# Five buffers instead of four for the weight tiles of a fused attention and feed-forward kernel

## The chip, the cores and the metric

The kernel runs on one core of a Trainium2 chip. The metric is the device time of one launch in microseconds (us); lower is better. Times of the kernel before are given as the median of three runs, and one further execution was recorded by the hardware profiler.

## What is computed

Two stages are fused. First, attention with 8 batches, 8 heads, 576 positions and a head width of 64, in which each query keeps only its 32 highest scores:

```python
scores = scale * np.matmul(q, k.transpose(0, 1, 3, 2))
kth = np.partition(scores, -top_k, axis=-1)[..., -top_k:-top_k + 1]
scores = np.where(scores >= kth, scores, -1000000000.0)
attn = np.exp(scores - np.max(scores, axis=-1, keepdims=True))
attn = attn / (np.sum(attn, axis=-1, keepdims=True) + 1e-09)
out = np.matmul(attn, v)
```

Then its output, regarded as 4608 tokens of width 512, goes through a gated feed-forward layer with an inner width of 1536:

```python
gate = 1.0 / (1.0 + np.exp(-(x @ w_gate)))
val = x @ w_val
return (gate * val @ w_out).astype(np.float32)
```

## The kernel before

**Attention.** The work is cut into steps: a batch, a pair of heads and a block of 128 queries (the last block of a head pair holds the 64 left-over positions of both heads). There are 160 steps. `scores` (line 221) lets TensorE multiply keys and queries into the PSUM tiles `pss` (L239, or L269 in batch 0), and ScalarE copies them to `s`. `select` (line 321) finds each row's 32nd highest score: VectorE takes maxima (L338, L342, L366) and writes the masked numerators `e` (L292). `turn` (line 371) transposes `e` on TensorE into `pt` (L378), 9 transposes of 128 columns for a full step. `weigh` (line 390) multiplies with the values into `po`: L414 and L424 write only half of the array's columns each (the tile `128*64` in the trace), one half per head, and L428 all of them (`128*128`). L431 adds the reciprocals of the sums, and the quotient is split into a high and a low part, `xh` and `xl`.

**Feed-forward.** Whenever the four head pairs of a unit of 256 or 384 tokens are there, `ffn` (line 451) queues tasks for it. `wide` (line 466) multiplies one 128-wide slice of `w_gate` and `w_val` with the tokens: 24 matmuls, L475 to L477, into two PSUM tiles `pz`. `narrow` (line 487) multiplies a slice of `w_out` in 12 matmuls, L496 to L498, into `po` (named `po2` in the program). A unit has 12 `wide` and 12 `narrow` tasks in three groups.

**Weights.** Each weight is kept as a high and a low part. `split_weights` (line 115) makes these parts once, for 18 tiles of 1 MB (8 KB in each of 128 partitions): VectorE and ScalarE prepare them, TensorE forms the remainder (`wrest`, L168 to L170), ScalarE writes it to the tile (`w_split`, L163 and L171), and SyncE writes the tile to device memory (`ws`, L172). The first two units use some of these tiles straight from on-chip memory; all others are read again by `load` in `ffn`:

```python
wt = pools["w"].tile([P, 2, 2, NP, P], F32R, tag="w", name=f"w_{nm0}_{idx}")
nc.sync.dma_start(wt.rearrange("p i a c n -> p i a (c n)").bitcast(F32), w_split[idx])
```

That is L461, 222 loads. Both `split_weights` and `load` take their tiles from the pool `w`, which `ffn_pools` (line 111) makes. A tile is handed out again when the last matmul that reads it is done, so the number of buffers sets how many weight tiles can be in use or under way.

**Order.** All engines run their instructions in order. The kernel writes steps and tasks in an order of its own (the loop in `run`), and the framework's scheduler then sorts the instructions of every engine by priority and by when it expects their operands and buffers to be ready. So a change of a pool's size can move instructions on every engine. SyncE issues nearly all DMAs in one queue: queries (L211, L208), keys (L192), values (L202), weights (L461) and outputs (L504); an issue that waits for a buffer holds up those behind it.

At the end a flag is formed on TensorE and VectorE (`n_bad`, L664, and `flag`, L666) and read by every engine (L667); only if it is set is everything computed again in a general way.

Of the kernel before, what the change touches and what calls it, by code (L numbers as in the profile page):

```python
# [30 lines left out]
def tile_topk_attention_then_gated_ffn(  # L31
# [19 lines left out]
    FG = NE = NP  # L51
# [57 lines left out]
    pools, fresh, copies, ahead, requests = {"first": bkr}, {}, [], [], []  # L109

    def ffn_pools():
        for name, bufs in (("w", 4), ("f2", 3), ("f4", NE), ("fg", FG + 1)):
            pools[name] = ctx.enter_context(tc.tile_pool(name=name, bufs=bufs))

    def split_weights():
# [401 lines left out]
    def run(general):  # L517
# [27 lines left out]
        if not general:  # L545
            ffn_pools()
            splits = split_weights()
# [176 lines left out]
```

## Time and profile before

| | |
|---|---|
| median of 3 runs | 1564.49 us |
| lowest, highest run | 1562.36, 1564.89 us |
| profiled execution, its own time | 1562.55 us |
| its span from first to last instruction | 1560.7 us |
| TensorE matmuls, busy | 1510.3 us (97%) |
| VectorE, busy | 1284.5 us (82%) |
| ScalarE, busy | 1116.0 us (72%) |
| GpSimd, busy | 1063.5 us (68%) |
| DMA queue q1, share of the 16 engines | 62.5% |
| granted TensorE clock, mean | 0.993 |

In the trace PE is the stream of matmuls on TensorE, PEld its weight loads, DVE VectorE, ACT ScalarE, POOL GpSimd, and SPq the DMA issues of SyncE. Matmuls follow each other in a pipeline, so that one's recorded time overlaps the next one's: the pace of TensorE is read from the distance between the starts of two matmuls, not from their durations.

### The profile page before, as it was taken

To read this page: it belongs to the slowest core of one execution; us is meant where nothing else is said; L and a number is where in the kernel's file an instruction comes from. 1 tells how busy PE (TensorE), PEld (TensorE's weight loads), DVE (VectorE), ACT (ScalarE), POOL (GpSimd) and SP (SyncE) were. 2 spreads that over 40 slices of the span, in tenths; PEclk is the share of its full clock that TensorE was granted. 3 is DMA by queue.
4 is the path that set the end of the run, shared out by engine and by line. 5 is a ranking of instruction groups with operands and counts; after the bars stand their busy time and mean duration, and the time that the engine had idled before them with its cause. 6 is when DMAs were issued, how large, how long until landed. Compare 5 with 4: busy or idle time off the path is not lost.

```text
span 1560.7 us, 33841 instructions
## 1 busy us (share of the span) xinstructions
PE 1510.3 (97%) x10586; PEld 1378.4 (88%) x10586; DVE 1284.5 (82%) x5806; ACT 1116.0 (72%) x2405; POOL 1063.5 (68%) x1756
## 2 busy tenths in 40 slices
PE   6779999999999999999999999999999999999998
PEld 2346689999999999899999999999999999999998
DVE  7999868999988789888988879988898888888311
ACT  8998968787877687776776766777777777677221
POOL 4666658898766786787666876787766886676211
PEclk8999999999999999999999999999999999999999
DMA  7763598887655755566555665565564675465574
GB/s 251 258 222 134 214 359 314 290 282 291 230 187 200 245 197 206 182 229 221 204 178 198 223 239 189 195 238 196 208 223 168 208 250 194 173 223 177 193 273 158
DMA packets 88894, 344.14 MB, mean 220 GB/s; under 512 B 9856, under 2 KB 36992, under 8 KB 57984
## 3 DMA queue, kind: packets, MB, share of 16 engines
q1 hardware_dynamic: 88560, 341.58, 62.5%
q8 instruction: 86, 1.41, 0.4%
q14 instruction: 104, 0.85, 0.2%
q10 hardware_dynamic: 144, 0.29, 0.1%
HBM read 313.52 MB, written 28.31 MB: 219 GB/s over the span
## 4 chain that ended last, share of the span: by engine, by line
PE 74%; DVE 9%; POOL 6%; ACT 6%; issue 2%; DMA 2%; SPq 0%; POOLq 0%; ACTq 0%
PE pz L476 11%; PE pz L477 11%; PE pz L475 11%; PE pss L239 8%; PE po L414 6%; PE pt L378 6%; PE po L496 5%; PE po L498 5%; PE po L497 5%; POOL u L356 3%; DVE cand L338 2%; DVE e L292 2%; PE po L428 2%; ACT e L287 2%; ACT under L350 1%
## 5 line engine op out<-in xcount | busy, mean ns | idle before, releaser
L356 POOL TENSOR_TENSOR u<-s,under 128x288 f32<-128x288 f32 x576 | 456.0, 814 | 138.1 <-ACT under L350 127.4
L338 DVE MAX8 cand<-s 128x8 f32<-128x72 f32 x2304 | 346.6, 217 | 64.6 <-ACT s L246 56.3
L475 PE MATMUL pz<-xh,w 128*128 128x384 f32 (+1 forms) x1184 | 390.4, 332 | 1.1 <-DVE acc L502 0.7
L477 PE MATMUL pz<-xh,w 128*128 128x384 f32 (+1 forms) x1184 | 391.1, 331 | 0.0
L476 PE MATMUL pz<-xl,w 128*128 128x384 f32 (+1 forms) x1184 | 390.1, 330 | 0.3 <-POOL xl L448 0.3
L292 DVE SCALAR_TENSOR_TENSOR e<-s,kths,e 128x576 f32<-128x576 f32 x288 | 280.7, 977 | 0.9 <-ACT e L287 0.7
L350 ACT ACTIVATE under<-s,leads 128x576 bf16<-128x576 f32 x288 | 222.6, 774 | 80.4 <-DVE leads L342 33.1
L366 DVE MAX8 kths<-u 128x8 f32<-128x584 f32 x288 | 219.1, 761 | 45.0 <-POOL u L357 43.3
L287 ACT ACTIVATE e<-s,st 128x576 f32<-128x576 f32 x288 | 209.6, 771 | 62.9 <-POOL st L346 62.4
L483 POOL TENSOR_TENSOR gl<-gf,gh 128x384 fp32r<-128x384 f32 (+1 forms) x156 | 151.6, 972 | 116.5 <-ACT gh L482 112.7
L475 PEld LDWEIGHTS pz<-xh,w 128*128 128x128 f32 x1184 | 222.8, 189 | 2.4 <-DVE acc L502 1.0
L476 PEld LDWEIGHTS pz<-xl,w 128*128 128x128 f32 x1184 | 223.3, 189 | 0.8 <-POOL xl L448 0.6
L477 PEld LDWEIGHTS pz<-xh,w 128*128 128x128 f32 x1184 | 223.1, 189 | 0.3
L379 ACT ACTIVATE et<-pt 128x384 f32<-128x384 f32 x384 | 177.9, 486 | 27.9 <-PE pt L378 26.0
L496 PE MATMUL po<-gh,w 128*128 128x384 f32 (+1 forms) x592 | 194.6, 334 | 0.7 <-DVE acc L502 0.6
L497 PE MATMUL po<-gl,w 128*128 128x384 f32 (+1 forms) x592 | 194.9, 330 | 0.0
L498 PE MATMUL po<-gh,w 128*128 128x384 f32 (+1 forms) x592 | 194.3, 330 | 0.0
L246 ACT ACTIVATE s<-pss 128x576 f32<-128x576 f32 x252 | 161.2, 640 | 41.3 <-PE pss L239 40.5
L378 PE MATMUL pt<-ident,e 128*128 128x128 f32 x1152 | 179.6, 274 | 7.9 <-ACT et L379 4.2
L239 PE MATMUL pss<-k,qh 128*128 128x288 f32 (+2 forms) x588 | 164.9, 298 | 1.5 <-ACT s L246 1.5
L378 PEld LDWEIGHTS pt<-ident,e 128*128 128x128 f32 x1152 | 140.9, 141 | 24.6 <-ACT et L379 6.4
L239 PE MATMUL pss<-k,ql 128*128 128x288 f32 (+2 forms) x588 | 159.9, 294 | 0.0
(108 smaller groups left out, 2897.3 us busy)
## 6 DMA issues: line engine op xcount, KB each, us to landing
w<-ws SPq DMA_DIRECT2D x222, 1024.0 KB, 5.0
v<-in_v_dram SPq DMA_DIRECT2D x68, 352.0 KB, 3.2
wraw<-in_w_dram SPq DMA_DIRECT2D x36, 512.0 KB, 4.9
ws<-w_split SPq DMA_DIRECT2D x18, 1024.0 KB, 4.6
qraw<-in_q_dram SPq DMA_DIRECT2D x140, 128.0 KB, 3.1
kraw<-in_k_dram SPq DMA_DIRECT2D x56, 288.0 KB, 4.0
out_dram<-acc SPq DMA_DIRECT2D x40, 192.0 KB, 4.8
out_dram<-acc SPq DMA_DIRECT2D x12, 128.0 KB, 5.3
```

What stands on the lines that cost most here:

```text
L239: nc.tensor.matmul(ps[:, half, o : o + n], x[:, h * P : (h + 1) * P], ks[h][:, k0 : k0 + n], start=t == 0, stop=t == len(todo) - 1,)
L287: nc.scalar.activation(e[:, j], s[:, j], AF.Exp, bias=st[:, j : j + 1], scale=1.0 / SHRINK)
L292: nc.vector.scalar_tensor_tensor(e[:, j], s[:, j], kth[j], e[:, j], op0=ALU.is_ge, op1=ALU.mult, accum_out=st[:, 4 + j : 5 + j])
L338: nc.vector.max(cand[:, j, 8 * g : 8 * g + 8], s[:, j, g * SEG : (g + 1) * SEG])
L356: nc.gpsimd.tensor_tensor(u[:, j, part], s[:, j, part], under[:, j, part], op=ALU.mult)
L378: nc.tensor.transpose(pt[:, c], ef[:, k0 : k0 + P], ident)
L475: nc.tensor.matmul(ps, wt[:, u, 0, d], xh, start=d == 0, stop=False)
L476: nc.tensor.matmul(ps, wt[:, u, 0, d], xl, start=False, stop=False)
L477: nc.tensor.matmul(ps, wt[:, u, 1, d], xh, start=False, stop=d == NP - 1)
L496: nc.tensor.matmul(ps, wt[:, e % 2, 0, f], gh, start=f == 0, stop=False)
L497: nc.tensor.matmul(ps, wt[:, e % 2, 0, f], gl, start=False, stop=False)
L498: nc.tensor.matmul(ps, wt[:, e % 2, 1, f], gh, start=False, stop=f == FG - 1)
```

## The change

```diff
     def ffn_pools():
-        for name, bufs in (("w", 4), ("f2", 3), ("f4", NE), ("fg", FG + 1)):
+        for name, bufs in (("w", 5), ("f2", 3), ("f4", NE), ("fg", FG + 1)):
             pools[name] = ctx.enter_context(tc.tile_pool(name=name, bufs=bufs))
```

The pool `w` gets a fifth buffer, 8 KB more in each partition. The scratch of the dynamic DMAs is 1024 bytes in both kernels (`dynamic_dma_scratch_size=1024`), so this line is the whole difference in the code. All engines have the same instructions before and after, 9464 on TensorE, 4945 on VectorE, 2121 on ScalarE, 1761 on GpSimd and 620 on SyncE on the path that is taken; the scheduler orders them differently.

SyncE, in the last batch but one, number 6 (`w` are weight loads, `qraw`, `kraw` and `v` loads of queries, keys and values, `ws` the split weights in device memory). Before:

```order
L211 DMA qraw_4_1_18468<-in_q_dram 128x256
L461 DMA w_9_19263<-ws_132 128x2048
L202 DMA v_0_18892<-in_v_dram 128x704
L211 DMA qraw_3_2_18619<-in_q_dram 128x256
L461 DMA w_10_19408<-ws_133 128x2048
L461 DMA w_11_19526<-ws_134 128x2048
L211 DMA qraw_4_2_18772<-in_q_dram 128x256
L461 DMA w_0_19671<-ws_123 128x2048
```

Now:

```order
L461 DMA w_9_19263<-ws_132 128x2048
L211 DMA qraw_4_1_18468<-in_q_dram 128x256
L461 DMA w_10_19408<-ws_133 128x2048
L461 DMA w_11_19526<-ws_134 128x2048
L211 DMA qraw_3_2_18619<-in_q_dram 128x256
L202 DMA v_0_18892<-in_v_dram 128x704
L461 DMA w_0_19671<-ws_123 128x2048
L211 DMA qraw_4_2_18772<-in_q_dram 128x256
```

The weight loads stand a place or two further ahead among the other loads.

TensorE, in `weigh` for queries 2 and 3 of head pair 0 in batch 0 (tile `po_3_0`; `pz_1_3` are the matmuls of the first feed-forward unit around it). Before, the eight half-column matmuls are one run:

```order
L170 MATMUL wrest_0_1462<-wt_frac_1455,plus 128x512
L414 MATMUL po_3_0_1676<-et_2_0_1526,v_0_1158 64x256 x8
L428 MATMUL po_3_0_1676<-et_2_0_1526,v_0_1158 128x256
L431 MATMUL po_3_0_1676<-ident,inv_2_0_1220 128x128
L431 MATMUL po_3_0_1676<-ident,inv_3_0_1316 128x128
```

Now they alternate with feed-forward matmuls, to the eighth:

```order
L414 MATMUL po_3_0_1676<-et_2_0_1526,v_0_1158 64x256
L475 MATMUL pz_1_3_0_1419<-xh_2_1061,w_split_1023 128x256
L414 MATMUL po_3_0_1676<-et_2_0_1526,v_0_1158 64x256
L476 MATMUL pz_1_3_0_1419<-xl_2_1062,w_split_1023 128x256
L414 MATMUL po_3_0_1676<-et_2_0_1526,v_0_1158 64x256
L477 MATMUL pz_1_3_0_1419<-xh_2_1061,w_split_1023 128x256
L414 MATMUL po_3_0_1676<-et_2_0_1526,v_0_1158 64x256
L475 MATMUL pz_1_3_0_1419<-xh_3_1237,w_split_1023 128x256
```

One run of eight has become eight runs of one.

TensorE, at the transposes of batch 5, block 1, head pair 3 (`pt_5_1_3`; `pss_5_3_0_1` are scores of a later step). Before:

```order
L477 MATMUL pz_8_0_0_1_15912<-xh_8_2_14188,w_8_0_15895 128x384
L378 MATMUL pt_5_1_3_0_15650<-ident_105,e_5_1_3_15246 128x128 x3
L378 MATMUL pt_5_1_3_1_15655<-ident_105,e_5_1_3_15246 128x128 x3
L239 MATMUL pss_5_3_0_1_15113<-k_11_0_1_13823,qh_5_3_0_14809 128x288
L239 MATMUL pss_5_3_0_1_15113<-k_11_0_1_13823,ql_5_3_0_14810 128x288
```

Now:

```order
L498 MATMUL po2_7_2_2_16146<-gh_7_2_3_15862,w_7_17_16144 128x384
L239 MATMUL pss_5_3_0_1_15113<-k_11_0_1_13823,qh_5_3_0_14809 128x288
L239 MATMUL pss_5_3_0_1_15113<-k_11_0_1_13823,ql_5_3_0_14810 128x288
L239 MATMUL pss_5_3_0_1_15113<-k_11_0_1_13823,qh_5_3_0_14809 128x288
L239 MATMUL pss_5_3_0_1_15113<-k_11_0_1_13823,ql_5_3_0_14810 128x288
L378 MATMUL pt_5_1_3_0_15650<-ident_105,e_5_1_3_15246 128x128 x3
L378 MATMUL pt_5_1_3_1_15655<-ident_105,e_5_1_3_15246 128x128
```

Other feed-forward work stands ahead of these transposes than before. Between the last score matmul of the step and its first transpose there were 94 matmuls, 59 of them feed-forward and 12 scores; now there are 83, with 44 and 16.

## Rows read from the trace of the kernel before

**Rows 1.** Stretches of 40 us: busy PE, PEld, DVE, ACT, POOL; clock; DMA share, GB/s.

```profile
120.00:160.00 40.00, 38.54 (x244) 27.11 (x242) 38.81 (x179) 35.27 (x73) 26.22 (x42) 1.00 0.39 130
160.00:200.00 40.00, 36.23 (x238) 27.42 (x237) 35.63 (x104) 36.51 (x66) 22.57 (x33) 1.00 0.55 205
200.00:240.00 40.00, 38.75 (x329) 34.69 (x329) 25.83 (x122) 24.22 (x55) 25.84 (x47) 1.00 1.01 384
...
1480.00:1520.00 40.00, 40.00 (x233) 40.00 (x232) 4.88 (x9) 8.33 (x17) 6.09 (x6) 1.00 0.77 267
```

**Rows 2.** Waits of PE: line, awaited engine and line; us in total, times, longest.

```profile
PE wrest L168 <- DVE wt_lead L153: 8.2, 7, 3.5
...
PE pss L269 <- DMA k<-in_k_dram: 4.1, 1, 4.1
PE pt L378 <- DVE e L292: 3.6, 6, 1.0
...
PE pz L477 <- ACT w_split L171: 1.6, 1, 1.6
```

**Rows 3.** Waits of SyncE's queue: the weight loads on feed-forward matmuls.

```profile
SPq L461 <- PE pz L477: 282.6, 97, 7.2
```

**Rows 4.** The weight tiles' page: the 222 loads, from issue to landing.

```profile
DMA to landing us min/median/max: 4.7/5.0/11.0
```

**Rows 5.** Timeline, 211 to 224 us: start, us, what.

```profile
211.78 6.08 SPq L461 DMA_DIRECT2D w<-ws  x4
...
223.40 0.28 PE L475 MATMUL pz<-xh,w 128*128 128x256 f32 x1
```

**Rows 6.** Timeline of PE, 131 to 134 us.

```profile
131.26 1.95 PE L414 MATMUL po<-et,v 128*64 128x256 f32 x16
133.14 0.70 PE L428 MATMUL po<-et,v 128*128 128x256 f32 x2
```

**Rows 7.** Timeline of PE, 871 to 873 us.

```profile
871.42 0.20 PE L239 MATMUL pss<-k,qh 128*128 128x64 f32 x1
871.55 0.65 PE L414 MATMUL po<-et,v 128*64 128x256 f32 x2
872.13 0.30 PE L239 MATMUL pss<-k,ql 128*128 128x64 f32 x1
872.36 1.08 PE L414 MATMUL po<-et,v 128*64 128x256 f32 x6
```

**Rows 8.** The chain that ended last, 120 to 215 us: start, us, what.

```profile
131.33 1.88 PE po L414 x16
...
163.77 0.94 ACT w_split L163
...
187.39 1.68 DVE wt_frac L162
```

**Rows 9.** Timeline, 985 to 1002 us: step of batch 5, block 1, head pair 3.

```profile
985.14 0.29 PE L239 MATMUL pss<-k,qh 128*128 128x288 f32 x1
985.27 0.30 PE L239 MATMUL pss<-k,ql 128*128 128x288 f32 x1
...
986.47 0.33 PE L476 MATMUL pz<-xl,w 128*128 128x384 f32 x1
986.64 0.33 PE L477 MATMUL pz<-xh,w 128*128 128x384 f32 x1
...
999.49 1.36 DVE L292 SCALAR_TENSOR_TENSOR e<-s,kths,e 128x576 f32<-128x576 f32 x1
...
1001.36 0.60 PE L378 MATMUL pt<-ident,e 128*128 128x128 f32 x4
...
1002.13 0.33 PE L378 MATMUL pt<-ident,e 128*128 128x128 f32 x1 [0.18 <-DVE e L292]
```

**Rows 10.** Timeline of SyncE at the end: the four last output DMAs.

```profile
1552.58 3.34 SPq L504 DMA_DIRECT2D out_dram<-acc  x4
```

## The prediction

> **What bounds the kernel now.** I read the stretches first. From 280 us to the end matmuls fill the time: the stretch of 1480 to 1520 us shows TensorE busy for 40.00 of 40 us, while VectorE needs 4.88 [rows 1]. Over the whole span TensorE is busy for 97%. So the time is the sum of TensorE's work at its pace plus the few places where it stands still. Between 120 and 240 us, where the weights are split and the first units start, it is idle for 1.46, 3.77 and 1.25 us, 6.5 in all [rows 1]. Before 120 us VectorE is the busier one; the two programs are alike there but for a few rows.
>
> Then I read what TensorE waits for [rows 2]. Of the DMAs it waits for one, a load of keys, 4.1 us, once. No weight load stands among its waits. The rest are short: 8.2 us on the preparation of the split weights, 3.6 us on masked numerators `e`, 1.6 us on a split tile.
>
> SyncE does wait for weight buffers: 97 times, 282.6 us in total, for the last matmul of an older tile [rows 3]. That is the wait that a fifth buffer shortens. The question is whether anybody on the path feels it.
>
> **The change part by part.**
>
> *The fifth buffer itself: 0 us.* A weight load takes 5.0 us in the median and 11.0 at most [rows 4]. The tightest one that I find, pairing the order of the loads with the first matmul on each tile, is issued at 211.78 us, the first of four in its row; even with the longest landing time it is there by 222.8 us, and its matmul starts at 223.40, right behind other matmuls [rows 5]. That is where the DMA engines are full, share 1.01 [rows 1]; later loads have more room. So loads issued one buffer earlier land earlier and wait in memory. What hides this term is the lead of four buffers that is already there. Queries and keys now stand a place or two further behind in SyncE's queue; they cost nothing as long as TensorE shows no wait on them, and it shows none but the 4.1 us at the start.
>
> *The eight half-column matmuls that now alternate with feed-forward matmuls, 3.6 us of TensorE.* This is what the scheduler does with the changed sizes, and it is the one place where TensorE's pace changes. I counted the runs of half-column matmuls in both programs: 82 before, 89 now, and all seven of the difference are here, where one run of eight became eight of one; elsewhere it is 81 and 81, in other places. In a run, eight such matmuls (16 in the trace, two passes each) take from 131.26 to 133.14 us, 1.88 us [rows 6]: two halves of the array work side by side. A lone one is to be seen at 871.55: the next matmul starts 0.58 us later, at 872.13, and the one after that, a matmul of 64 columns, is followed after 0.23 us, where its like at 871.42 is followed after 0.13 [rows 7]. So a lone one costs 0.58 + 0.10 = 0.68 us, eight of them 5.44, and 5.44 − 1.88 = 3.6 us more.
>
> How much of this reaches the end? At 131 us the chain that ended last runs through TensorE, through this very run, but at 164 us through ScalarE and at 187 us through VectorE [rows 8], and TensorE has 6.5 us of idle time there to lose [rows 1]. The ends are 0 (all taken out of that idle time) and 3.6 (none, since ScalarE and VectorE wait for TensorE in turn). The chain is on TensorE for about as much of this stretch as on the others, so I take half: **+1.8 us**.
>
> The Trainium skill, "TensorE: Matmul & The Clock Gate", section "Single matmul latency", gives a constant of about 166 ns at the full clock for a matmul that can't hide its drain, and "TensorEngine Tiling (Array Packing)", section "Key Properties", says that a change of the tiling mode drains the array. By these, seven more runs would cost an estimated 1.2 us, a third of what the rows give; halved, the sum below would be 1.2 us smaller. The lone run at 871.55 agrees that there is a drain; it shows besides that a half without its partner costs time, and I go by it.
>
> *Transposes that come nearer to their scores: +0.8 us.* TensorE can transpose `e` only when VectorE, ScalarE and GpSimd have finished the selection. In the step of the third order excerpt the last scores start at 985.27 us, the numerators of the first head are done at 999.49 + 1.36 = 1000.85, and the first transpose starts at 1001.36, 0.5 us later; the fifth, of the second head, waits 0.18 us [rows 9]. Now 15 fewer feed-forward matmuls lie between, at 0.17 us (986.47 to 986.64), and 4 more scores at 0.13 us (985.14 to 985.27): 2.6 − 0.5 = 2.1 us less, and with 0.5 us in hand a wait of 1.6 us. The same sum over all 160 steps finds ten that fall short, the first at 122 us and the last at 1381, the worst being this one; together 7 us. They come in five clusters of neighbouring steps, and as VectorE runs on while TensorE waits, I count only the worst of each: 4.4 us. From this the 3.6 us that TensorE waits for `e` now [rows 2] go off, as those steps have got more room. The ends are −3.6 (no such wait is left, and none comes) and +7.
>
> *The end: 0 us.* SyncE now reads the flag behind the last weight load and ahead of the four last output DMAs. The first of these starts at 1552.58 [rows 10], and the flag's matmul now stands some 40 matmuls ahead of the program's end; it is done before.
>
> **The sum.** 0 + 1.8 + 0.8 + 0 = +2.6 us. The profiled execution took 1562.55 us, so its like would take 1565.2. It lies 1.9 us under the median of the three runs; against the median of 1564.49 the sum is **1567.1 us**, 0.17% more. About 0.2%, 3.1 us, is what a measurement of this kernel can tell from no change.
>
> **The rivals.**
>
> *The waits count in full (slower).* The lone half-column matmuls are on the path with all of their 3.6 us, and the nearer transposes bring 7 us of waits of which the present ones make up only a quarter, 1.8. This gives 3.6 + 7 − 1.8 = +8.8, 1573.3 us. For it speaks that TensorE has next to no idle time after 280 us in which a delay could vanish; against it, that VectorE is busy for only 82% and catches up. It decides once the steps that fall short lie too far apart to help each other, some 40 us or more.
>
> *The fifth buffer frees the start (faster).* Split tiles and their reloads share the pool; if the splitting is held by it, TensorE's idle time of 6.5 us between 120 and 240 us [rows 1] shrinks to about 2 and the interleaving is hidden with it: −4.5, 1560.0 us. For it speaks the wait of 8.2 us on preparations and of 1.6 us on a split tile [rows 2]; against it, that most of the former ends before the pool is full and none of them names a buffer.
>
> *Nothing reaches the end.* The interleaving goes into idle time and the new waits equal the old: 0, 1564.5 us.
>
> **How the numbers follow.** The forecast has a chance of 0.45. Its own range is 1563 to 1569, of which two thirds lie below 1567.6, where 0.2% ends. The slower rival has 0.25, the faster 0.17, nothing 0.13. So faster by over 0.2% is 0.17; within 0.2% is 0.30 + 0.13 = 0.43; slower is 0.15 + 0.25 = 0.40. The range goes from the faster rival's time, 1560, to just over the slower one's, 1574; the rest of their chances lies outside.
>
> **What would show it.** In the new profile the stretch of 125 to 140 us should hold eight short rows of L414, each followed after some 0.6 us; TensorE should still show no wait on a weight load; SyncE's wait on feed-forward matmuls should fall; waits on `e` should be listed near batch 5, blocks 1, head pairs 2 and 3. I am wrong if TensorE's idle time between 120 and 240 us falls by more than 4 us without new waits later, if waits of TensorE appear on other lines and add up to more than 5 us, or if the start before 120 us moves.

## The result and the profile after

The changed kernel takes **1583.97 us** (median of four runs, 1583.87 to 1585.81), against 1564.69 us for the kernel before on the same chip. The ratio is 1.0128, with an interval of 1.0112 to 1.0143: 19.3 us slower. The prediction was 1567.1 us, its range ended at 1574. The sign was the second likeliest, the size is outside. The profiled execution took 1584.06 us, its span is 1582.2 us.

The stretches that answer to [rows 1], and one long stretch from 280 us to 1480 us, in the kernel after:

```profile
120.00:160.00 40.00, 38.12 (x227) 26.25 (x228) 36.39 (x157) 32.05 (x67) 26.80 (x41) 1.00 0.31 112
160.00:200.00 40.00, 36.28 (x237) 27.05 (x235) 37.75 (x127) 35.54 (x68) 24.67 (x36) 1.00 0.61 221
200.00:240.00 40.00, 38.27 (x293) 33.71 (x292) 21.43 (x96) 23.41 (x50) 19.62 (x37) 1.00 0.93 365
280.00:1480.00 1200.00, 1185.28 (x8526) 1119.52 (x8526) 1024.99 (x4783) 865.04 (x1926) 879.39 (x1470) 1.00 0.61 211
1480.00:1520.00 40.00, 40.00 (x253) 38.85 (x253) 6.88 (x14) 7.83 (x17) 7.97 (x8) 1.00 0.70 241
```

The long stretch in the kernel before:

```profile
280.00:1480.00 1200.00, 1196.26 (x8639) 1133.09 (x8638) 1026.45 (x4749) 866.99 (x1923) 875.09 (x1464) 1.00 0.62 214
```

TensorE is idle between 120 and 240 us for 1.88 + 3.72 + 1.73 = 7.3 us, against 6.5 before. But where it stood still for 3.7 us in 1200, it now does for 14.7. The place that looked safe, because it was full, is where the time went.

TensorE's waits in the whole run after the change, the lines of [rows 2]:

```profile
PE wrest L168 <- DVE wt_lead L153: 5.8, 6, 2.0
PE pt L378 <- DVE e L292: 4.8, 7, 1.2
PE pss L239 <- ACT s L246: 4.7, 6, 1.7
PE pss L269 <- DMA k<-in_k_dram: 4.1, 1, 4.1
...
PE pz L477 <- ACT w_split L171: 1.9, 2, 1.2
```

Again no weight load is among them. The line in the middle, score matmuls that wait for ScalarE to copy an earlier tile `pss` to `s` and so to free its PSUM buffer, isn't in [rows 2]; before the change it read

```profile
PE pss L239 <- ACT s L246: 1.5, 3, 0.8
```

SyncE's wait of [rows 3] after the change:

```profile
SPq L461 <- PE pz L477: 272.1, 91, 7.4
```

It was 282.6 us; the fifth buffer hardly shortens it.

**Where the time came from.** Both kernels hold the same 9464 instructions on TensorE. So I number them in each program's order and read when the 250th, 500th, 1919th, 2967th and 9460th start: equal counts are nearly equal work, and the stretches can be laid beside each other. Up to the 250th TensorE's order is the same in both. Four stretches of the kernel before, between these instructions (columns as in [rows 1]):

```profile
114.00:163.04 49.04, 46.13 (x296) 32.90 (x294) 47.61 (x220) 42.34 (x89) 32.77 (x51) 1.00 0.45 150
163.04:361.44 198.40, 192.92 (x1559) 173.83 (x1559) 169.09 (x765) 155.92 (x349) 153.73 (x257) 1.00 0.81 295
361.44:517.22 155.78, 155.33 (x1161) 148.09 (x1160) 137.19 (x648) 115.88 (x257) 112.02 (x190) 1.00 0.62 217
517.22:1554.45 1037.23, 1033.94 (x7221) 980.98 (x7221) 825.56 (x3756) 699.45 (x1541) 700.53 (x1164) 1.00 0.60 208
```

The same four after the change:

```profile
116.14:168.54 52.40, 49.29 (x301) 33.87 (x299) 48.79 (x220) 42.45 (x90) 34.44 (x54) 1.00 0.37 128
168.54:371.46 202.92, 194.16 (x1553) 175.40 (x1554) 166.81 (x732) 153.29 (x343) 150.68 (x250) 0.99 0.81 297
371.46:528.68 157.22, 156.48 (x1161) 148.12 (x1160) 140.06 (x674) 116.60 (x259) 115.69 (x192) 1.00 0.62 215
528.68:1575.89 1047.21, 1036.55 (x7221) 982.72 (x7221) 819.49 (x3759) 697.18 (x1541) 703.15 (x1165) 1.00 0.60 205
```

Length less busy time is TensorE's idle time. By subtraction:

```
instructions   longer   of it busy   of it idle
250-500          +3.4        +3.2         +0.2
500-1919         +4.5        +1.2         +3.3
1919-2967        +1.4        +1.2         +0.3
2967-9460       +10.0        +2.6         +7.4
sum             +19.3        +8.2        +11.1
```

The sum is what the medians show. (The two profiled executions differ by 2.1 us more, in the first 250 instructions; that part varies between executions, as shown below.)

**The first row is the alternation.** TensorE's timeline from 128 us, after the change (start, us, what; as in [rows 6]):

```profile
128.07 0.28 PE L477 MATMUL pz<-xh,w_split 128*128 128x256 f32 x1
128.19 0.28 PE L475 MATMUL pz<-xh,w_split 128*128 128x256 f32 x1
...
130.08 0.65 PE L414 MATMUL po<-et,v 128*64 128x256 f32 x2
130.65 0.39 PE L475 MATMUL pz<-xh,w_split 128*128 128x256 f32 x1
130.97 0.65 PE L414 MATMUL po<-et,v 128*64 128x256 f32 x2
131.54 0.38 PE L476 MATMUL pz<-xl,w_split 128*128 128x256 f32 x1
131.86 0.65 PE L414 MATMUL po<-et,v 128*64 128x256 f32 x2
...
137.24 0.59 PE L428 MATMUL po<-et,v 128*128 128x256 f32 x2
```

A lone half-column matmul holds TensorE for 0.57 us (130.08 to 130.65), the matmul behind it for 0.32 (130.65 to 130.97), a pair for 0.89. A matmul like the latter in a run takes 0.12 (128.07 to 128.19), so a lone one costs 0.89 − 0.12 = 0.77 us, near the 0.68 that was worked out from [rows 7]. From 130.08 to 137.24 us, where the next full-width matmul with the values starts, there are the eight and nine feed-forward matmuls: 7.16 us, where one run of eight and the nine would take 1.88 + 9 × 0.12 = 2.96. That is 4.2 us more on the spot.

**The last row is waits.** TensorE's waits from 528.68 us on, after the change (awaited engine and line, us in total, times, longest):

```profile
PE pss L239 <- ACT s L246: 3.4, 3, 1.7
PE pt L378 <- DVE e L292: 2.8, 4, 1.2
PE pt L378 <- DVE leads L342: 1.1, 1, 1.1
PE po L414 <- ACT et L379: 1.0, 1, 1.0
PE po L496 <- DVE acc L502: 0.8, 2, 0.6
```

With two of 0.7 us that are left out here they make 10.5 us in thirteen places. Before, all waits of that stretch make 3.2 us in seven places, and these two lines of them are small:

```profile
PE pss L239 <- ACT s L246: 0.2, 1, 0.2
PE pt L378 <- DVE e L292: 0.2, 1, 0.2
```

The line that names `leads` is a transpose as well. Here are VectorE's numerators ahead of it and the transpose itself:

```profile
898.11 1.38 DVE L292 SCALAR_TENSOR_TENSOR e<-s,kths,e 128x576 f32<-128x576 f32 x1
...
899.64 0.52 PE L378 MATMUL pt<-ident,e 128*128 128x128 f32 x3 [1.13 <-DVE leads L342]
```

It reads `e` and not `leads`, and these numerators end at 898.11 + 1.38 = 899.49, 0.15 us ahead of it; the profile put the wait down to a short instruction of VectorE right behind them. So the transposes wait 2.8 + 1.1 = 3.9 us for numerators, 3.7 more than before. The score matmuls wait 3.4 us for ScalarE to empty a PSUM tile, 3.2 more than before. These two make 6.9 of the 7.3 us by which the waits of the stretch have grown.

### The profile page after: what moved, and what is told of

Same layout as the page of the kernel before. It is cut to its first block, busy times and chain, and to the rows that moved or that the text cites. A ratio compares the mean times of both kernels' runs of the same rounds, so it can differ in the third digit from the quotient of the medians.

```text
span 1582.2 us, 33814 instructions
## 1 busy us (share of the span) xinstructions
PE 1523.6 (96%) x10586; PEld 1385.4 (88%) x10586; DVE 1280.7 (81%) x5806; ACT 1113.0 (70%) x2405; POOL 1067.6 (67%) x1756
## 4 chain that ended last, share of the span: by engine, by line
PE 35%; DVE 7%; POOL 5%; ACT 3%; issue 1%; POOLq 0%; ACTq 0%; DVEq 0%
PE pz L476 5%; PE pz L477 5%; PE pz L475 5%; PE pss L239 3%; PE po L496 3%; PE po L497 3%; PE po L498 3%; POOL u L356 3%; PE pt L378 3%; PE po L414 2%; DVE cand L338 2%; DVE kths L366 2%; DVE e L292 2%; ACT e L287 1%; POOL k L196 1%
## 5 line engine op out<-in xcount | busy, mean ns | idle before, releaser
L483 POOL TENSOR_TENSOR gl<-gf,gh 128x384 fp32r<-128x384 f32 (+1 forms) x156 | 154.9, 993 | 125.0 <-ACT gh L482 121.2
```

## The experiments

The theory after the result was that the time is lost by the order into which the scheduler sorts the instructions, and that the buffer itself gives and takes nothing. The rivals were that the buffer itself costs something (its memory, or loads that start earlier and get in the way of others), and that a shortage of weight tiles is what an additional buffer moves elsewhere. All times below stand beside runs of the kernel before on the same chip, with a median of 1564.33, 1564.16 or 1564.02 us, by the group of runs.

The stretches of all profiles, in us between TensorE's n-th instructions, as above:

```
               250-661  661-1919  1919-2967  2967-9460   250-9460   first 250
before            84.0     163.5      155.8     1037.2     1440.5       114.0
after             87.0     168.3      157.2     1047.2     1459.8       116.1
b4_pad            83.7     163.6      155.9     1038.1     1441.2       116.3
l42_1             84.8     163.4      155.8     1037.8     1442.0       116.6
s18_1             87.2     163.5      155.8     1037.6     1444.1       115.1
s18_2             80.8     164.6      156.0     1037.5     1438.9       115.0
s18_2_again       81.0     164.6      156.0     1037.6     1439.2       114.1
b4_weigh400       83.0     164.9      156.9     1037.6     1442.4       115.3
b4_miles          84.2     165.0      155.3     1047.5     1452.0       113.6
b5_miles          87.3     167.0      155.7     1047.8     1457.7       114.9
b5_weigh400       80.8     164.7      158.7     1040.2     1444.5       116.5
b4_raise190       83.3     163.5      155.8     1036.7     1439.3       115.5
b5_raise190       85.0     164.7      157.1     1037.1     1444.0       114.6
b3                82.2     165.6      156.2     1047.9     1451.9       121.9
```

### The memory alone

Four buffers, and a tile of 8 KB per partition that nothing uses, so that memory is as full as in the changed kernel. TensorE, VectorE, ScalarE and SyncE keep the order of before; GpSimd has one instruction more, at the start.

```diff
+    spare_room = const.tile([P, 2048], F32, tag="spare_room", name="spare_room")
+    nc.gpsimd.memset(spare_room[:, :1], 0.0)
...
-        for name, bufs in (("w", 5), ("f2", 3), ("f4", NE), ("fg", FG + 1)):
+        for name, bufs in (("w", 4), ("f2", 3), ("f4", NE), ("fg", FG + 1)):
```

> Four buffers, and a spare tile of 8 KB per partition in the room that the fifth buffer takes; TensorE, VectorE, ScalarE and SyncE have the very order of the kernel before. If the order of the instructions alone makes the time: 1564.5 us, within 3. If the room matters (other tiles lie at other addresses): towards 1584 us.

Measured: 1565.63 us, ratio 1.0005 (0.9994 to 1.0016). The room costs nothing.

### The fifth buffer alone, in the order of before

The first 42 weight tiles share four buffers, and from the 43rd on every fifth tile gets a fifth one, from a pool of its own. With this, TensorE, VectorE, ScalarE and GpSimd run in exactly the order of before; SyncE issues weight loads earlier.

```diff
+        for name, bufs in (("w", 4), ("w5", 1), ("f2", 3), ("f4", NE), ("fg", FG + 1)):
...
+    def weight_tile(name):
+        n = len(weights)
+        weights.append(name)
+        fifth = n >= 42 and n % 5 == 4
+        return pools["w5" if fifth else "w"].tile([P, 2, 2, NP, P], F32R, tag="w5" if fifth else "w", name=name)
...
-            wt = pools["w"].tile([P, 2, 2, NP, P], F32R, tag="w", name=f"w_{nm0}_{idx}")
+            wt = weight_tile(f"w_{nm0}_{idx}")
```

> Five buffers from the 43rd weight tile on, four before. TensorE, VectorE, ScalarE and GpSimd have the order of the kernel before from the first instruction to the last; only SyncE issues its weight loads earlier. If the order alone makes the time and the fifth buffer is worth nothing by itself: 1564.5 us, within 3, with SyncE's wait for feed-forward matmuls clearly under 282 us. If loads that are issued earlier cost by themselves (crowded DMA engines, queries and keys behind them): 1570 us or more. If they help by themselves: under 1561.

Measured: 1565.03 us, ratio 1.0001 (0.9991 to 1.0010). So from about 300 us on, where the load of the 42nd tile is issued, the fifth buffer by itself is worth nothing in either direction. Between the splitting and that time no kernel here has it in the order of before. One part of the expectation failed: SyncE's wait (this kernel has six lines more, so that L461 is L467 here) did not fall clearly under 282 us:

```profile
SPq L467 <- PE pz L483: 279.2, 99, 7.2
```

A reason that fits, argued and not shown by itself: SyncE fills whatever buffers there are and then waits for one to come free, so how long it waits per tile is set by the pace at which TensorE uses tiles up, not by their number.

### The late order, with four buffers

Two numbers of the table by which the loop in `run` sets how many feed-forward tasks have to be out are raised by 8, with four buffers.

```diff
-    MILES = [(512, 256), (832, 512), (1152, 768), (1536, 1152), (1984, 1536), (2624, 2112)]
+    MILES = [(512, 264), (832, 520), (1152, 768), (1536, 1152), (1984, 1536), (2624, 2112)]
...
-        for name, bufs in (("w", 5), ("f2", 3), ("f4", NE), ("fg", FG + 1)):
+        for name, bufs in (("w", 4), ("f2", 3), ("f4", NE), ("fg", FG + 1)):
```

> Four buffers; two entries of the table that paces the feed-forward tasks are 8 tokens higher, which re-sorts all engines' orders from the first unit on and changes no work. If any re-sorted order loses (the order before was a lucky one, and the fifth buffer is innocent): 1572 to 1590 us, with TensorE's idle time after 280 us at 8 to 15 us instead of 3.7. If the fifth buffer itself is what costs: 1564.5 us, within 5.

Measured: 1574.77 us, ratio 1.0067 (1.0044 to 1.0089). This is the run that decides. From TensorE's 2967th instruction to the end its order is that of the changed kernel, instruction by instruction, and ScalarE's, VectorE's and GpSimd's are too; only SyncE's differs, as it has a buffer less. The stretch takes 1047.5 us, the changed kernel's 1047.2, that of before 1037.2. All thirteen waits of the changed kernel stand there again, at the same instructions, beside one more of 0.16 us. After the change, TensorE between 1018 and 1034 us (the idle time before a row and its releaser in brackets):

```profile
1020.50 0.66 PE L378 MATMUL pt<-ident,e 128*128 128x128 f32 x4 [1.21 <-DVE e L292]
...
1026.54 1.95 PE L414 MATMUL po<-et,v 128*64 128x256 f32 x16 [0.98 <-ACT et L379]
...
1033.85 0.40 PE L239 MATMUL pss<-k,qh 128*128 128x288 f32 x1 [1.75 <-ACT s L246]
```

With four buffers, the same instructions ten microseconds earlier:

```profile
1010.43 0.66 PE L378 MATMUL pt<-ident,e 128*128 128x128 f32 x4 [1.23 <-DVE e L292]
...
1016.74 1.95 PE L414 MATMUL po<-et,v 128*64 128x256 f32 x16 [1.25 <-ACT et L379]
...
1023.77 0.40 PE L239 MATMUL pss<-k,qh 128*128 128x288 f32 x1 [1.46 <-ACT s L246]
```

Half of the 19 us thus needs no fifth buffer; it needs the order.

The third of these waits shows how a delay on another engine reaches TensorE. ScalarE's timeline after the change:

```profile
1029.82 1.45 ACT L287 ACTIVATE e<-s,st 128x576 f32<-128x576 f32 x2 [2.79 <-POOL st L346]
...
1033.17 0.63 ACT L246 ACTIVATE s<-pss 128x576 f32<-128x576 f32 x1
```

ScalarE stands 2.79 us for `st` from GpSimd, the row maxima with their sign turned (L346). It then has exponentials, a copy of the reciprocals, a count and the high part of some queries ahead of the copy `s`, which ends at 1033.17 + 0.63 = 1033.80, and the score matmul starts at 1033.85. Such a wait is on no list of transposes.

### The same table, with five buffers

The same two numbers in `MILES`, in the changed kernel. TensorE gets an order that is neither that of before nor that of the change, with 103 runs of half-column matmuls (before 82, the change 89).

> Five buffers, with the same two entries higher: another order again, with 103 runs of half-column matmuls (82 before, 89 after). If the order alone decides: anywhere from 1570 to 1595 us, and about 0.5 us for each of the 14 further runs on top of the waits. If the fifth buffer costs by itself: 1584 us, within 5, and about 20 above the run with four buffers and the same entries.

Measured: 1580.68 us, ratio 1.0106 (1.0086 to 1.0126). This lies in both ranges; but it is 6 us above the run with four buffers and the same table, not the 20 that a cost of the buffer by itself would have shown. The late stretch takes 1047.8 us, the stretch with the alternation 87.3. The 0.5 us for each of the 14 further runs don't show: the kernel is no slower than the changed one.

### Without the alternation, with five buffers

`weigh` raises the priority of its matmuls by 200 places (`RAISE`). In batch 0 it now does so by 400, and the eight half-column matmuls stay together: 82 runs.

```diff
-                queued.enter_context(tc.high_priority(offset=RAISE))
+                queued.enter_context(tc.high_priority(offset=RAISE if nm[:2] != "0_" else 2 * RAISE))
```

> Five buffers; in batch 0 alone the matmuls with the values have twice the priority. The alternation at 130 us is gone (82 runs). If that alternation costs 3 to 4 us that reach the end: TensorE gets from its 250th to its 500th instruction in 49.5 us as before, not in 52.5. The rest is re-sorted again: by the order theory the total lies between 1570 and 1590 us; if the alternation were the main cause of the loss, it lies under 1570.

Measured: 1569.25 us, ratio 1.0030 (1.0018 to 1.0042), just under 1570 and so, by the letter of the expectation, on the side of the alternation as the main cause. It isn't that: TensorE gets from its 250th to its 500th instruction in 48.6 us, where the changed kernel needs 52.4, and the larger part of the gain is elsewhere, as the rest was sorted anew as well: the late stretch takes 1040.2 us instead of 1047.2. This run alone doesn't tell the alternation's price.

### The alternation, with the order of before behind it

Every fifth of the 18 split tiles gets the fifth buffer, and all tiles behind them share four: `fifth = n < 18 and n % 5 == 4` in `weight_tile`, which hands out the tile in `split_weights` as well. TensorE's order is that of the change up to the 661st instruction, alternation included, and that of before from there on.

```diff
+        fifth = n < 18 and n % 5 == 4
...
-                wt = pools["w"].tile([P, 2, 2, NP, P], F32R, tag="w", name=f"w_split_{idx}")
+                wt = weight_tile(f"w_split_{idx}")
```

> Five buffers only for the 18 tiles of the splitting, four afterwards. Up to its 661st instruction TensorE has the order of the changed kernel, with the alternation at 130 us, and from there to the end that of the kernel before. If each stretch costs what its own order makes it cost: 3 us more in instructions 250 to 500, nothing later, 1567.5 us, within 2.5. If a disturbance at the start is what makes the later waits: 1575 us or more.

Measured: 1568.68 us, ratio 1.0029 (1.0019 to 1.0038), as expected: 4.5 us by the medians. The profile shows 3.2 us more than before between 250 and 661, and nothing behind: 163.5, 155.8 and 1037.6 us, against 163.5, 155.8 and 1037.2. So what is lost there is carried to the end. Other instructions of this stretch have changed places too; that it is the alternation that costs is borne out by all kernels side by side. Between the 250th and the 500th instruction the four with the alternation take 52.4 to 52.9 us, all others 47.1 to 49.9, and the five of them that have the order of before there 48.4 to 49.9.

### The fifth buffer at the start, without the alternation

The same, with the doubled priority of batch 0. TensorE has the order of before from the 1919th instruction on.

> Five buffers only for the splitting, and in batch 0 twice the priority for the matmuls with the values, so that they don't alternate; from TensorE's 1919th instruction to the end the order of the kernel before. The run with five buffers throughout and this priority took 158.3 us for TensorE's instructions 250 to 1250, the kernel before 163.6. If that gain comes from the order of this stretch, it stays: 1560 us, within 3. If it was bought with the later waits: 1564 to 1568.

Measured: 1562.40 us, ratio 0.9991 (0.9982 to 1.0001), within what was expected if the gain stays. The stretch of 250 to 661 takes 80.8 us, 3.2 less than before; 1.1 us are given back up to the 1919th instruction. To settle its sign it ran again in another group:

> The same kernel as s18_2, in more rounds, to settle whether it is faster than the kernel before. TensorE's instructions from the 250th to the end took 1438.9 us there and 1440.5 in the kernel before. If that difference is real: a ratio of 0.9990, with an interval under 1. If it is chance: an interval around 1.

Measured: 1562.04 us, ratio 0.9986 (0.9977 to 0.9995), so it is faster than both kernels, by 0.14% against the kernel before, less than the 0.2% that the prediction took as what a measurement here can tell; the two groups of runs agree. Where it comes from is one stretch: TensorE between its 500th and 661st instruction, before the change,

```profile
163.04:197.96 34.92, 31.15 (x196) 22.47 (x195) 30.87 (x92) 32.03 (x59) 19.53 (x31) 1.00 0.56 203
```

and in this kernel,

```profile
162.78:195.01 32.23, 30.30 (x190) 22.46 (x188) 29.34 (x88) 30.21 (x56) 20.10 (x28) 1.00 0.67 240
```

TensorE's idle time there falls from 3.8 to 1.9 us. The missing alternation isn't what brings this: with five buffers and `RAISE` at 190 (below) the alternation is there, and the stretch of 500 to 661 takes 32.1 us too.

### The doubled priority with four buffers

> Four buffers, and the same doubled priority in batch 0; the order differs from that before only in TensorE's instructions 451 to 2692. If the gain of 5 us in the splitting is the priority's: instructions 250 to 1250 in 158 to 160 us and a total near 1560. If it needs the fifth buffer: 163 to 164 us for them, and a total of 1564.5, within 4.

Measured: 1565.78 us, ratio 1.0010 (1.0000 to 1.0019). The change is that of the doubled priority, with four buffers. The stretch of 250 to 661 takes 83.0 us, so that the doubled priority by itself doesn't give the 80.8 above. All kernels with 32 us between 500 and 661 have a fifth buffer among the split tiles; whether they need the buffer or only the order that comes with it isn't separated here.

### Three buffers

> Three buffers. A load then leads its first matmul by one tile less, some 6 us: from a median of 12.8 us between landing and first use to about 6.5, and at 200 to 240 us, where the tightest of before had 2.3 us, to nothing. If four buffers are enough and no more than enough: waits of TensorE on weight loads appear for the first time, 5 to 20 us in all, nearly all of them between 200 and 260 us, and the time is 1575 to 1600 us with the re-sorted order. If the lead is ample even then: no wait names a weight load, and the time lies between 1565 and 1585.

Measured: 1581.89 us, ratio 1.0114 (1.0098 to 1.0129), with `("w", 3)`, a time that lies in both ranges. The waits for weight loads that were expected are not there, but for one, the only one in all of these profiles:

```profile
PE pz L475 <- DMA w<-ws: 0.9, 1, 0.9
```

A tile lies loaded for 6.0 us (median) before its first matmul, 12.8 with four buffers and 19.4 with five. So even three buffers nearly suffice for the loads. What is slower are the start, 121.9 us for the first 250 instructions (argued, not shown: because the 18 split tiles share the pool), and once more the late stretch, 1047.9 us.

### Another order, with four buffers and with five

`RAISE` is 190 instead of 200, once with four buffers and once with five.

```diff
-    RAISE = 200
+    RAISE = 190
```

> Four buffers; the matmuls with the values are raised by 190 places instead of 200. TensorE's order is that of before up to its 4147th instruction and another one behind it. If another order loses by its own waits, buffers or not: instructions 250 to 4147 in the time of before, within 1 us, and 2 to 10 us lost behind them, 1567 to 1575 us. If only five buffers lose: 1564.5, within 2.5.

> Five buffers, the same 190. The alternation at 130 us is there (87 runs), the order behind it is yet another. If the order alone decides: 3.5 us lost in instructions 250 to 500, and the rest somewhere between 0 and 20 us, 1567 to 1588. If five buffers always lose the same: 1584, within 4.

Measured with four: 1562.74 us, ratio 0.9990 (0.9981 to 0.9999). A loss was expected, and it didn't come: TensorE's order differs from that of before in most places from the 4147th instruction on, and the late stretch takes 1036.7 us. Another order isn't worse as such. By itself this run fits the rival that only five buffers lose; the run with four buffers and the late order speaks against that, and so does the next one. Measured with five: 1567.58 us, ratio 1.0023 (1.0014 to 1.0033), and its late stretch takes 1037.1 us, so a fifth buffer doesn't bring the late loss with it.

## Why the prediction was wrong

**The fifth buffer itself: right, as far as it was tried.** 0 us was predicted; in the order of before, from about 300 us on, it measured 1.0001, and its memory 1.0005. The reason given, the lead that is there, was right too, and three buffers show how much there is to spare. But the reading of [rows 3] as "the wait that a fifth buffer shortens" was wrong: 282.6 us became 272.1, and 279.2 in the order of before.

**The alternation: price nearly right, absorption wrong.** 3.6 us of TensorE were predicted; the rows show 4.2 on the spot, and between the 250th and the 500th instruction 3.4 are left. The price came from one lone matmul in the trace of before. The Trainium skill's constant ("TensorE: Matmul & The Clock Gate", "Single matmul latency") had given an estimated 1.2 us by the prediction's working; the trace disagrees with it by a factor of three here. Half was to vanish in idle time. Next to nothing did: in that stretch TensorE's busy time rose by 3.2 us and its idle time by 0.2. The failed step is "the chain is on TensorE for about as much of this stretch as on the others, so I take half". What came out is the upper end of that term, and the kernel with the alternation and the order of before behind it shows it at the end of the run: 4.5 us by the medians, an interval of 0.19% to 0.38%, some 3 to 6 us, and so not 1.8. That the other engines' work there waits for TensorE in turn, so that each stall moves with it, is the reason that the prediction gave for that end; it fits, but no run shows it apart.

The alternation was also called "the one place where TensorE's pace changes". It isn't. The count of runs, 81 and 81 elsewhere, doesn't say how long they are. After the change four half-column matmuls of batch 6 stand alone among scores:

```profile
1246.52 0.43 PE L414 MATMUL po<-et,v 128*64 128x128 f32 x2
1246.88 0.37 PE L239 MATMUL pss<-k,qh 128*128 128x224 f32 x1
1247.18 0.43 PE L414 MATMUL po<-et,v 128*64 128x128 f32 x2
```

Each holds TensorE for 0.36 us and the score matmul behind it for 0.30, where one of 288 columns among its like takes 0.13 [rows 9]. This is in the late stretch, and so in its 2.6 us of busy time, which are otherwise not divided here.

**The transposes: the new waits right, what goes off wrong, and only half of the late waits.** Waits on `e` were to rise from 3.6 us to 4.4; they rose to 4.8, or 5.9 with the one that is put down to `leads`. The worst step was to wait 1.6 us and waits 1.21. The new waits were counted at 4.4 us, and 3.9 stand in the late stretch. The step that failed in this term is that "the 3.6 us that TensorE waits for `e` now [rows 2] go off": ahead of the 2967th instruction 3.4 of them stood, and 2.0 still do. So the term measured +2.3 us instead of +0.8.

**What had no term: the other waits.** The prediction summed one relation of the order, from scores to the transposes, over all 160 steps. It did not sum the others, without giving a reason: among them the PSUM tiles that another engine has to empty first. The largest is the score matmuls' wait for ScalarE to copy `pss` to `s`; over the whole run it rose from 1.5 to 4.7 us, and in the late stretch from 0.2 to 3.4. This and the transposes make 6.9 of the 7.3 us by which the waits of the late stretch grew. The prediction named the sign that would show it, waits "on other lines" of more than 5 us.

Together the prediction had +2.6 us where 19.3 were measured. The late stretch takes 10.0 of them and the alternation 3.4; the 5.9 us between them stay open.

**The end: right.** 0 us; nothing between the last matmuls and the end of the span differs by more than 0.1 us.

**The rivals.** "The waits count in full" had the right sign, and it was right that a full TensorE has next to no idle time in which a delay could vanish. Its 3.6 us for the alternation came out; its 5.2 us for transposes were more than the 2.3 measured. At +8.8 us it was too small, as it too held no other waits. The rival in which the start gets faster is real, but in other orders: with a fifth buffer and another priority of the matmuls with the values, 2.7 to 2.8 us between instructions 500 and 661.

**What stays open.** The 4.5 us between instructions 500 and 1919 were not reproduced with four buffers. After the change the trace shows two waits there,

```profile
325.28 0.55 PE L378 MATMUL pt<-ident,e 128*128 128x128 f32 x3 [1.02 <-ACT et L379]
327.25 0.39 PE L496 MATMUL po<-gh,w 128*128 128x256 f32 x1 [1.43 <-DVE acc L502]
```

and right behind them 3.4 us at the lower of TensorE's two clocks, 1.2 GHz, which cost some 1.5 us (feed-forward matmuls of 256 columns follow each other there after 0.21 us instead of 0.12). The other kernels with five buffers for all tiles lose 1.2 to 3.5 us between 661 and 1919, and so do two with four buffers and another order there, by 1.4 and 1.5 us. That the rest is order too is argued, not shown. This stretch lies between 198 and 361 us before the change, where the DMA engines are full for a time (share 1.01 in [rows 1]), and up to about 300 us of it the fifth buffer wasn't tried in the order of before: that loads which are issued earlier cost something there isn't ruled out. The 1.4 us between 1919 and 2967 are open as well. Nor is it shown what makes one of the scheduler's orders good and another bad.

## What to carry to other kernels

Where a framework sorts the instructions, a change of a pool's size can change every engine's order: price the new order by all of its relations (operands, and buffers that must first be emptied), and not by the one that is easiest to sum, and try the resource apart from the order, as with the pool of its own here. A full engine has no idle time in which a delay could hide, and here the idle time of a busy start hid next to none of one either, so take a delay there as reaching the end in full unless a row shows otherwise. A queue that waits for buffers is no sign that it needs more of them: look at how long what it loads lies there before it is used.

## What was not expected of the hardware

The same order gives the same time closely: 1047.2 and 1047.5 us for 6493 matmuls of two programs with a different number of buffers. The start doesn't: with the order of before the first 250 instructions took 114.0, 116.3 and 116.6 us in three profiles, at a granted clock of 0.93, 0.87 and 0.86 in the first 120 us.

Two waits of 1.02 and 1.43 us, with 0.5 us of work between them, were followed by a fall of the granted clock. The stretch behind them, after the change:

```profile
328.00:332.00 4.00, 4.00 (x23) 4.00 (x22) 3.80 (x27) 0.78 (x4) 1.65 (x4) 0.57 0.71 172
```

The clock stands at 0.57 there with TensorE busy for all of the time, while before the change it was at 1.00 from 120 us on, except at the very end. So a short wait can cost more than its length. Other waits as long, such as those at 1020 and 1033 us, were followed by no such fall. Nor does the order of the instructions alone decide it. The kernel with the fifth buffer for the split tiles and the doubled priority has two profiles, s18_2 and s18_2_again. In both TensorE waits 0.72 us and then 0.74, the second time up to 219.80 us in one and up to 218.97 us in the other. The stretch behind them, in the first and in the second:

```profile
220.00:224.00 4.00, 4.00 (x36) 3.92 (x33) 3.93 (x32) 3.23 (x8) 3.61 (x7) 0.59 1.01 422
220.00:224.00 4.00, 4.00 (x35) 4.00 (x34) 3.86 (x30) 3.83 (x9) 3.69 (x7) 1.00 1.01 418
```
